# Weights made on VectorE in a fixed plan, with raw words two pieces ahead, in a fused attention and Fourier mixing kernel

## The chip, the cores and the metric

The kernel runs on one core of one Trainium2 chip. The metric is the time of one execution in device microseconds; lower is better. Before the change the median of three runs is 930.02 us (928.06 to 930.32).

## The reference

```python
def _attn_ref(q, k, v):                     # (4, 8, 768, 64) each
    block, window = (32, 16)
    scale = 1.0 / np.sqrt(D)
    k_sum = k.reshape(B, H, nb, block, D).max(axis=3)
    v_sum = v.reshape(B, H, nb, block, D).mean(axis=3)
    scores_l = scale * np.matmul(q, k.transpose(0, 1, 3, 2))
    mask_l = np.abs(pos[:, None] - pos[None, :]) < window
    scores_s = scale * np.einsum('bhsd,bhnd->bhsn', q, k_sum) + np.log(block)
    ...
    return np.matmul(softmax, np.concatenate([v, v_sum], axis=2))

def _moe_ref(x, w_ch1, w_ch2):              # x (4, 768, 512)
    mixed = np.real(np.fft.fft(np.fft.fft(x, axis=1), axis=2))
    u = x + mixed
    un = (u - mean(u)) / np.sqrt(var(u) + 1e-06)
    ch = np.maximum(un @ w_ch1, 0.0) @ w_ch2
    return u + ch                           # w_ch1 (512, 2048), w_ch2 (2048, 512)
```

The output of the attention, with the heads side by side, is the x of the mixing. The two weight matrices are stored as 64-bit floats; q, k and v are fp32.

## The kernel before, in words

There are four batches. For each one the kernel runs an attention (generator `gen_attention`, four pairs of heads), a Fourier stage (`gen_fourier`) and a channel stage (`gen_channel`). The attention of the next batch runs beside the Fourier and channel stages of the present one: `drive` (L956) takes steps from several generators in turn and so sets the order in which instructions are recorded; a scheduler then sets the order on each engine. Engines work through their own order, and so does SP, whose queue issues nearly all transfers.

**Attention.** `load` (L534) brings q and k of a head pair, 128 tokens to a tile, token p of tile t on partition p, so each packet is 64 floats. `prepare` (L582) transposes them on PE (L590) and copies them out of PSUM on ACT (L591). `scores` and `values` do the windowed part; `load_values` (L559) brings the windows of v, and on every second pair starts `block_sums` (L543), which brings the blocks of v and adds them on POOL through `gtt` (L528, its instructions carry L529).

**Fourier stage.** Additions on DVE fold x into the tile `fold`; matmuls with cosine and sine tables give y (L786), copied out by ACT (L792) and DVE (L793); matmuls mx (L806, L808) finish the transform; DVE adds x and takes mean and variance; an integer guess and four Newton steps give the inverse root (L823); DVE makes un (L833); PE transposes it (L837) into u, copied by DVE and ACT in turn (L838).

**Channel stage.** Both matrix products use a seven-product scheme of the Strassen kind: each operand is cut into four blocks, and four sums of blocks are added to it, so that a weight slab has seven parts (`_left_sums` L456 and `_right_sums` L463 make the sums). There are eight left slabs (w1, from w_ch1) and eight right slabs (w2, from w_ch2). In two chunks of four, `gen_channel` (L844) first makes h for each slab j (matmuls hx, hy, hz on L863; copies on ACT L870, L876, L878; additions on DVE through `tt`, L525, whose instructions carry L526; relu on DVE L867 and ACT L888), then multiplies h and its sums s with four right slabs for three pairs of row tiles (ox, oy, oz on L906, additions to x on DVE).

**Weights.** Batch 0 makes the slabs; batches 1 to 3 fetch them. `convert` (L678) turns 64-bit words into fp32, a half slab (a piece) at a time: it brings the raw words (L683; the tag raw has two buffers), takes exponent and mantissa apart on DVE (L687, L688), scales both on ACT (L689, L690), joins sign and low word on DVE (L691, L693), and multiplies the two parts on POOL. `make_w1` and `make_w2` convert two pieces, make the four sums on POOL and store the slab in DRAM (L706, L717), from where `get_w1` and `get_w2` (L722, L727) fetch it in later batches. `gen_weights` (L730) goes through four left slabs, four right ones, the other four left and the other four right. Three slabs are recorded after the whole attention of batch 0, the other thirteen beside its Fourier and channel stages, one slab to every four steps of those.

## Time and profile before

| | |
|---|---|
| median of 3 runs | 930.02 us |
| the profiled execution's own time | 931.02 us |
| its span in the profile | 929.2 us |
| mean granted TensorE clock | 0.94 |
| busy: PE, DVE, ACT, POOL | 829.2, 530.3, 168.8, 147.4 us |
| moved by DMA | 122.76 MB in 127,917 packets |

Engines: PE is TensorE's matmul, PEld its weight load, DVE VectorE, ACT ScalarE, POOL GpSimd, SP the queue of transfers. A group's row gives line, engine, operation, output<-inputs by the program's names, partitions x elements, the count, then total busy us and mean ns, and after the next bar the idle time before them with what ended it. A row of waits gives total us, times, and the longest. A row of windows gives, for one stretch, each engine's busy us with its instructions, the granted clock, the DMA share and GB/s.

### The profile page before, as it was taken

How to read it: one execution, taken by the hardware profiler on the slowest of the kernel's cores; microseconds unless marked ns; L12 is line 12 of the kernel's file. 1: busy time of each engine (PE TensorE's matmuls, PEld its weight loads, DVE VectorE, ACT ScalarE, POOL GpSimd, SP SyncE). 2: the span in 40 equal slices, each digit the busy share in tenths (PEclk: the TensorE clock that was granted, in tenths of full speed). 3: DMA queues.
4: the chain of work that ended last, by engine and by line, in shares of the span. 5: the costliest groups of instructions: out<-in, count | busy, mean ns of one | idle time of the engine just before them, and what ended most of it. 6: DMA issues, size and time to landing. Idle time of an engine off the chain costs nothing.

```text
span 929.2 us, 15289 instructions
## 1 busy us (share of the span) xinstructions
PE 829.2 (89%) x6386; PEld 618.3 (67%) x6386; DVE 530.3 (57%) x1158; ACT 168.8 (18%) x349; POOL 147.4 (16%) x142
## 2 busy tenths in 40 slices
PE   4778748687886799999999999999999997999997
PEld 3656634466753588657875888668857875587586
DVE  1366986799368964935423937635327556352252
ACT  2222312432023102221112012220021011200200
POOL 2230625567056700020000000000000000000000
PEclk9777859989898999999999999999999998999999
DMA  9995791777926508826162147321051161213101
GB/s 187 178 189 164 236 178 62 219 228 218 163 76 244 199 35 287 151 97 147 35 206 78 57 150 232 86 80 41 27 197 60 46 261 54 105 41 153 45 24 48
DMA packets 127917, 122.76 MB, mean 132 GB/s; under 512 B 102912, under 2 KB 111328, under 8 KB 127840
## 3 DMA queue, kind: packets, MB, share of 16 engines
q1 hardware_dynamic: 127296, 121.14, 46.9%
q8 instruction: 52, 0.85, 0.4%
q10 hardware_dynamic: 544, 0.56, 0.2%
q14 instruction: 25, 0.20, 0.1%
HBM read 100.71 MB, written 20.97 MB: 131 GB/s over the span
## 4 chain that ended last, share of the span: by engine, by line
PE 68%; DVE 20%; DMA 4%; POOL 3%; issue 3%; SPq 2%; ACT 1%; DVEq 0%; ACTq 0%; POOLq 0%
PE ox L906 17%; PE hx L863 15%; PE oz L906 8%; PE hz L863 7%; PE oy L906 4%; PE hy L863 4%; PE y L786 3%; DMA raw<-in_moe_w_ch_dram 2%; DVE cvt L688 2%; POOL w L529 2%; DVE cvt L693 2%; PE sc L606 2%; DVE cvt L691 2%; DVE x L526 2%; DVE cvt L687 2%
## 5 line engine op out<-in xcount | busy, mean ns | idle before, releaser
L863 PE MATMUL hx<-u,w 128*128 128x384 f32 x512 | 189.2, 500 | 15.5 <-ACT h L876 6.0
L863 PEld LDWEIGHTS hx<-u,w 128*128 128x128 f32 x512 | 97.9, 195 | 85.8 <-ACT h L876 8.9
L906 PE MATMUL ox<-w,h 128*128 128x256 f32 x384 | 93.9, 393 | 8.4 <-DVE x L526 7.9
L863 PE MATMUL hz<-u,w 128*128 128x384 f32 x256 | 96.6, 498 | 4.7 <-ACT h L878 4.7
L906 PE MATMUL ox<-w,s 128*128 128x256 f32 x384 | 92.8, 384 | 4.0 <-DVE x L526 3.5
L906 PE MATMUL oz<-w,s 128*128 128x256 f32 x384 | 93.0, 384 | 2.6 <-DVE s L526 2.6
L906 PEld LDWEIGHTS ox<-w,h 128*128 128x128 f32 x384 | 75.4, 197 | 22.8 <-DVE x L526 9.1
L906 PEld LDWEIGHTS ox<-w,s 128*128 128x128 f32 x384 | 72.0, 191 | 16.3 <-DVE x L526 5.6
L526 DVE TENSOR_TENSOR x<-ox,x 128x256 f32<-128x256 f32 x96 | 40.4, 422 | 74.2 <-PE ox L906 74.2
L906 PEld LDWEIGHTS oz<-w,s 128*128 128x128 f32 x384 | 73.3, 192 | 13.1 <-DVE s L526 2.9
L863 PEld LDWEIGHTS hz<-u,w 128*128 128x128 f32 x256 | 49.8, 195 | 40.3 <-POOL vb L529 5.3
L529 POOL TENSOR_TENSOR w<-cvt 128x512 f32<-128x512 f32 x32 | 43.6, 1364 | 133.2 <-DVE cvt L693 72.5
L529 POOL TENSOR_TENSOR w<-w 128x256 f32<-128x256 f32 x64 | 56.2, 893 | 3.1
L526 DVE TENSOR_TENSOR h<-hy,h 128x384 f32<-128x384 f32 x32 | 17.8, 555 | 67.5 <-PE hy L863 67.5
L526 DVE TENSOR_TENSOR h<-hx,h 128x384 f32<-128x384 f32 x32 | 17.8, 555 | 56.1 <-PE hx L863 56.0
L863 PE MATMUL hy<-u,w 128*128 128x384 f32 x128 | 46.5, 486 | 0.0
L906 PE MATMUL oy<-w,h 128*128 128x256 f32 x192 | 46.0, 380 | 0.3 <-POOL w L529 0.3
L606 PEld LDWEIGHTS sc<-qt,kt 64*64 64x64 f32 x1536 | 33.7, 157 | 12.7 <-issue 8.6
L606 PE MATMUL sc<-qt,kt 64*64 64x32 f32 x1536 | 36.7, 239 | 6.0 <-issue 3.7
L906 PEld LDWEIGHTS oy<-w,h 128*128 128x128 f32 x192 | 36.5, 191 | 5.8 <-POOL w L529 0.7
L867 DVE TENSOR_SCALAR h<-h 128x384 f32<-128x384 f32 x96 | 38.7, 404 | 2.9
L526 DVE TENSOR_TENSOR s<-h 128x512 f32<-128x512 f32 x48 | 39.2, 816 | 0.2
(92 smaller groups left out, 1043.3 us busy)
## 6 DMA issues: line engine op xcount, KB each, us to landing
w<-dw SPq DMA_DIRECT2D x48, 896.0 KB, 5.6
raw<-in_moe_w_ch_dram SPq DMA_DIRECT2D x32, 512.0 KB, 5.1
dw<-w SPq DMA_DIRECT2D x16, 896.0 KB, 4.3
vw<-in_v_dram SPq DMA_DIRECT2D x62, 192.0 KB, 5.7
kn<-in_k_dram SPq DMA_DIRECT2D x32, 192.0 KB, 5.3
qn<-in_q_dram SPq DMA_DIRECT2D x32, 192.0 KB, 5.2
vb<-in_v_dram SPq DMA_DIRECT2D x16, 384.0 KB, 6.3
out_dram<-x SPq DMA_DIRECT2D x24, 256.0 KB, 2.0
```

The source lines that it names most:

```text
L526: nc.vector.tensor_tensor(out=out, in0=in0, in1=in1, op=op)
L529: nc.gpsimd.tensor_tensor(out=out, in0=in0, in1=in1, op=op)
L606: nc.tensor.matmul(ps[h][r:r + 64, i, :], kt[rows, o:o + 64], qt[rows, o:o + BLOCK], start=True, stop=True)
L687: nc.vector.tensor_scalar(out=ex, in0=high, scalar1=0x7FF00000, scalar2=None, op0=ALU.bitwise_and)
L688: nc.vector.tensor_scalar(out=man, in0=high, scalar1=0x000FFFFF, scalar2=None, op0=ALU.bitwise_and)
L691: nc.vector.scalar_tensor_tensor(out=ex, in0=high, scalar=-(1 << 31), in1=ex, op0=ALU.bitwise_and, op1=ALU.bitwise_or)
L693: nc.vector.scalar_tensor_tensor(out=tmp[:, 1, :], in0=low, scalar=2.0 ** -52, in1=tmp[:, 1, :], op0=ALU.mult, op1=ALU.add)
L786: nc.tensor.matmul(y, fgs[par][:, st, P * g:P * (g + 1)], fs[par][:, g % 2, st, :], start=(st == 0), stop=(st == HT - 1))
L863: nc.tensor.matmul(ps, w[:, a, kk, :], u[:, r, kk, :], start=start and kk == 0, stop=stop and kk == 1, skip_group_check=True)
L867: nc.vector.tensor_scalar(out=t, in0=t, scalar1=0.0, scalar2=None, op0=ALU.max)
L906: nc.tensor.matmul(ps, left[a][:, n, :], wt[2, b, j][:, r, :], start=start and n == 0, stop=stop and n == NC - 1, skip_group_check=True)
```

## The change

The multiplication that ends a conversion and the four sums of each slab go from POOL to DVE. The sixteen slabs follow a written plan; some entries wait for a named step of the channel stage to be recorded. Raw words go through four buffers, which v's blocks share, and are loaded up to two pieces ahead of the piece in work. Left slabs are made in place; right slabs 0 to 3 are made in four small buffers of the tag s, stored, and fetched again when the channel stage of batch 0 comes to them. Weight steps now run beside the attention of batch 0 as well.

Around it: q and k are loaded with six consecutive tokens on a partition, one transfer for both heads, three pairs ahead, with twice as many copies on ACT behind the transposes; v's blocks are loaded one pair earlier; the two divisions per half in `values` become one; the second copy of y goes to ACT; the inverse root takes three shorter Newton steps; every second un goes to ACT; the first three left slabs of a batch are fetched in the Fourier stage; in batch 0 the relus go to ACT.

```diff
     def load(b, g):
-        qn, kn = (apool.tile([P, NST, 2, D], FP, tag="nat", bufs=4, name=f"{n}n_{b}_{g}") for n in "qk")
+        qn, kn = (apool.tile([P, 2, NST * D], FP, tag="nat", bufs=4, name=f"{n}n_{b}_{g}") for n in "qk")
         for dst, src in ((kn, k), (qn, q)):
-            for e in range(2):
-                nc.sync.dma_start(out=dst[:, :, e, :], in_=src[b, 2 * g + e].rearrange("(t p) d -> p t d", p=P))
+            nc.sync.dma_start(out=dst, in_=src[b, 2 * g:2 * g + 2].rearrange("e (p t) d -> p e (t d)", p=P))
...
-        raw = [bpool.tile([4 * nb, hf, D], FP, tag="vb", bufs=2, name=f"vb_{b}_{gg}_{i}") for i in range(2)]
+        raw = [bpool.tile([4 * nb, hf, D], FP, tag="raw", bufs=4, name=f"vb_{b}_{gg}_{i}") for i in range(2)]
...
-            for h in range(2):
-                ps = abank([P, HT, P], f"qk_{b}_{g}_{h}")
+            for e in range(2):
+                ps = abank([P, S2], f"qk_{b}_{g}_{e}")
                 for i in range(HT):
-                    nc.tensor.transpose(ps[:, i, :], src[:, HT * h + i].rearrange("p e d -> p (e d)"), ident)
-                nc.scalar.copy(out=dst[:, S2 * h:S2 * (h + 1)], in_=ps.rearrange("p i c -> p (i c)"))
+                    nc.tensor.transpose(ps[:, i::HT], src[:, e, P * i:P * (i + 1)], ident)
+                for par in range(2):
+                    nc.scalar.copy(out=dst[D * e:D * (e + 1), par:S:2], in_=ps[D * par:D * (par + 1)])
...
+    plan = [(1, 0, False, None), (1, 1, False, None), (2, 0, True, None), (1, 2, False, None), (2, 1, True, None),
...
+    def load_raw(upto):
+        for f, j, hh in pieces[len(raws):upto]:
+            raw = bpool.tile([P, 2 * HD, 2], I32, tag="raw", bufs=4, name=f"raw_{f}_{j}_{hh}")
...
+    def convert(piece, dst):
+        i = pieces.index(piece)
+        load_raw(i + 3)
+        raw = raws[i]
...
-        gtt(dst, vb, va, ALU.mult)
+        tt(dst, tmp[:, 1, :], tmp[:, 0, :], ALU.mult)
+        yield
...
+    def make(f, j, staged):
+        if staged:
+            t = [bpool.tile([P, n, HD], FP, tag="s", bufs=5, name=f"m{f}_{j}_{i}") for i, n in enumerate((2, 2, 2, 1))]
...
-        _left_sums(gtt, lambda i: w[:, i])
-        nc.sync.dma_start(out=dw1[j], in_=w)
+            yield from convert((f, j, hh), pair(hh).rearrange("p a n -> p (a n)"))
+        (_left_sums if f == 1 else _right_sums)(tt, part)
+        yield
...
-                nc.vector.tensor_copy(out=tr[:, g, par:S2:2], in_=ps[:, F2:0:-1])
+                nc.scalar.copy(out=tr[:, g, par:S2:2], in_=ps[:, F2:0:-1])
...
-            for _ in range(4):
-                tt(z, y, y, ALU.mult)
+            for _ in range(3):
+                nc.vector.scalar_tensor_tensor(out=z, in0=y, scalar=-0.5, in1=y, op0=ALU.mult, op1=ALU.mult)
                 tt(z, z, var, ALU.mult)
...
+            if t % 2:
+                nc.scalar.activation(out=un[:, t, :], in_=x[:, t, :], func=AF.Identity, bias=shift[:, i:i + 1],
+                                     scale=y[:, i:i + 1])
...
                 def relu(t):
-                    nc.vector.tensor_scalar(out=t, in0=t, scalar1=0.0, scalar2=None, op0=ALU.max)
+                    if b:
+                        nc.vector.tensor_scalar(out=t, in0=t, scalar1=0.0, scalar2=None, op0=ALU.max)
+                    else:
+                        nc.scalar.activation(out=t, in_=t, func=AF.Relu)
...
-    drive((gen_attention(0), 1))
+    attn, weights = gen_attention(0), gen_weights()
+    drive((first(attn, 5), 1), (first(weights, 15), 3))
     get_tables(0)
-    drive((gen_weights(0, 3), 1))
+    drive((attn, 1), (first(weights, 21), 3))
     for b in range(B):
-        gens = [(gen_post(b), 4)]
+        attn = gen_attention(b + 1) if b + 1 < B else iter(())
         if b == 0:
-            gens.append((gen_weights(3, None), 1))
-        if b + 1 < B:
-            gens.append((gen_attention(b + 1), 1))
-        drive(*gens)
+            drive((gen_fourier(0), 4), (first(weights, 20), 4), (first(attn, 5), 1))
+            drive((gen_channel(0), 4), (weights, 12), (attn, 1))
+        else:
+            drive((gen_post(b), 4), (attn, 1))
```

In the changed kernel the DVE lines of a conversion are L714, L715, L719 and L721, the ACT lines L716 and L717; transfers are L701 (raw), L749 and L752 (stores of staged and in-place slabs), L766 and L773 (fetches). `drive` now spreads the steps of its generators evenly over a round.

More of the change, by code (lines that the diff above doesn't have):

```diff
@@ L720, in get_w1, with gen_weights @@
+    def gen_weights():
+        for f, j, staged, stage in plan:
+            while stage and stage not in issued:
+                yield
+            yield from make(f, j, staged)
     def get_w1(b, j):
         w = bpool.tile([P, 7, 2, P], FP, tag="w1", bufs=3, name=f"w1_{b}_{j}")
+        if b == 0 and (1, j) not in made:
+            return
         nc.sync.dma_start(out=w, in_=dw1[j])
@@ L726, in get_w2 @@
         w = bpool.tile([P, 7, HD], FP, tag="w2", bufs=NC, name=f"w2_{b}_{j}")
+        if b == 0 and (2, j) not in made:
+            return
         nc.sync.dma_start(out=w, in_=dw2[j])
         wt[2, b, j] = w
-    def gen_weights(first, last):
-        steps = [(f, j) for c in range(0, NJ, NC) for f in (make_w1, make_w2) for j in range(c, c + NC)]
-        for f, j in steps[first:last]:
-            f(j)
-            yield
     tables = {}
```

129 lines of the change are left out of this document (81 added, 48 removed).

## The prediction

> **What bounds the kernel now.** I read the page's engine totals and its forty slices first, then the windows by stage, then who waits for whom inside the slowest stage.
>
> ```profile
> span 929.2 us, 15289 instructions
> PE 829.2 (89%) x6386; PEld 618.3 (67%) x6386; DVE 530.3 (57%) x1158; ACT 168.8 (18%) x349; POOL 147.4 (16%) x142
> ...
> PE   4778748687886799999999999999999997999997
> ...
> PEclk9777859989898999999999999999999998999999
> ```
>
> PE is the bound over the span, but not evenly: from slice 15 on it is full, and before that it is neither full nor at full clock. The windows are cut at the end of the first batch's attention (60), at the first channel matmul (137), at the first Fourier matmul of batches 1 to 3 (351, 550, 745) and at the end.
>
> ```profile
> core 0: us, PE busy (x) PEld busy (x) DVE busy (x) ACT busy (x) POOL busy (x), PEclk, DMA share, GB/s
> 0.00:60.00 60.00, 39.74 (x975) 32.45 (x976) 16.77 (x57) 15.39 (x33) 13.48 (x18) 0.86 1.04 184
> 60.00:137.00 77.00, 53.08 (x629) 43.12 (x629) 63.79 (x148) 21.50 (x43) 28.06 (x27) 0.67 0.81 196
> 137.00:351.00 214.00, 176.53 (x939) 123.52 (x939) 164.02 (x255) 50.54 (x92) 100.02 (x92) 0.92 0.55 158
> 351.00:550.00 199.00, 195.27 (x1575) 146.42 (x1574) 104.97 (x254) 31.55 (x71) 5.86 (x6) 1.00 0.46 127
> 550.00:745.00 195.00, 193.14 (x1584) 144.33 (x1583) 102.04 (x256) 29.98 (x67) 0.00 (x0) 1.00 0.33 106
> 745.00:929.00 184.00, 171.43 (x692) 128.47 (x690) 78.72 (x193) 19.81 (x43) 0.00 (x0) 0.97 0.24 92
> ```
>
> Batches 1 to 3 hold 3.7 + 1.9 + 12.6 us in which PE is idle; little can be won there. The first 351 us are the stage that can move. Its channel mixing is measured against that of batch 1, by the first channel matmul (hx) and the first Fourier matmul of the next batch (y):
>
> ```profile
> 137.21 1.67 PE L863 MATMUL hx<-u,w 128*128 128x384 f32 x4
> 350.62 1.48 PE L786 MATMUL y<-fs,fold 128*128 128x193 f32 x8
> 389.29 1.46 PE L863 MATMUL hx<-u,w 128*128 128x384 f32 x4
> 549.03 1.48 PE L786 MATMUL y<-fs,fold 128*128 128x193 f32 x8
> ```
>
> That is 213.4 us in batch 0 against 159.7 us in batch 1 for the same matmuls and the same share of the next batch's attention. So 53.7 us of batch 0's channel stage are the price of making the weights beside it. Who is waited for there, PE first, then the DMA queue, then DVE:
>
> ```profile
> PE ox L906 <- DVE x L526: 11.3, 4, 3.8
> PE hx L863 <- ACT h L876: 6.0, 2, 4.0
> ```
> ```profile
> SPq L717 <- POOL w L529: 48.2, 8, 10.7
> SPq L706 <- POOL w L529: 47.5, 5, 17.9
> ```
> ```profile
> DVE cvt L687 <- DMA raw<-in_moe_w_ch_dram: 9.1, 3, 4.4
> DVE cvt L687 <- POOL w L529: 3.4, 2, 1.7
> ```
>
> PE waits for additions and copies on DVE and ACT, which stand in line behind conversions. The DMA queue spends 95.7 us of the 214 waiting for POOL's sums before a store, with the next raw words behind it. POOL also slows DVE itself. Of the four conversion operations on DVE the trace gives minimum, median and maximum:
>
> ```profile
> L687 DVE TENSOR_SCALAR cvt<-raw x32: 412/587/1485, 85.8 to 311.8; 128x512 int32<-128x512 int32 x32
> L688 DVE TENSOR_SCALAR cvt<-raw x32: 413/946/1502, 86.2 to 312.2; 128x512 int32<-128x512 int32 x32
> L691 DVE SCALAR_TENSOR_TENSOR cvt<-raw,cvt x32: 669/680/2835, 87.2 to 313.1; 128x512 int32<-128x512 int32 x32
> L693 DVE SCALAR_TENSOR_TENSOR cvt<-raw,cvt x32: 677/679/2836, 87.8 to 313.7; 128x512 f32<-128x512 uint32 x32
> ```
>
> The fast ones stand where POOL is idle, the slow ones where it computes. The same operation of 0.41 us takes up to 1.5.
>
> **The change part by part.** First the work that goes from POOL to DVE.
>
> ```profile
> L529 POOL TENSOR_TENSOR w<-w 128x256 f32<-128x256 f32 x64 | 56.2, 893 | 3.1
> L529 POOL TENSOR_TENSOR w<-cvt 128x512 f32<-128x512 f32 x32 | 43.6, 1364 | 133.2 <-DVE cvt L693 72.5
> L689 ACT ACTIVATE cvt<-cvt,rebias 128x512 int32<-128x512 int32 x32 | 23.1, 722 | 82.7 <-DVE cvt L687 82.6
> L690 ACT ACTIVATE cvt<-cvt 128x512 f32<-128x512 int32 x32 | 20.0, 626 | 7.3 <-DVE cvt L688 5.0
> L526 DVE TENSOR_TENSOR x<-ox,x 128x256 f32<-128x256 f32 x96 | 40.4, 422 | 74.2 <-PE ox L906 74.2
> ```
> The next two views are groups by form on DVE, in batch 1 (POOL nearly idle) and in 137 to 351:
> ```profile
> L526 DVE TENSOR_TENSOR s<-h 128x512 f32<-128x512 f32 x12 | 8.2, 684 | 0.1
> ```
> ```profile
> L691 DVE SCALAR_TENSOR_TENSOR cvt<-raw,cvt 128x512 int32<-128x512 int32 x24 | 23.0, 959 | 0.4 <-ACT cvt L689 0.4
> L688 DVE TENSOR_SCALAR cvt<-raw 128x512 int32<-128x512 int32 x24 | 22.8, 951 | 0.0
> L693 DVE SCALAR_TENSOR_TENSOR cvt<-raw,cvt 128x512 f32<-128x512 uint32 x24 | 20.9, 869 | 0.0
> L687 DVE TENSOR_SCALAR cvt<-raw 128x512 int32<-128x512 int32 x24 | 17.9, 744 | 12.4 <-DMA raw<-in_moe_w_ch_dram 9.1 <-POOL w L529 3.4
> L526 DVE TENSOR_TENSOR s<-h 128x512 f32<-128x512 f32 x12 | 14.6, 1214 | 0.0
> L867 DVE TENSOR_SCALAR h<-h 128x384 f32<-128x384 f32 x24 | 12.8, 539 | 0.5
> ```
>
> A piece costs DVE (23.0+22.8+20.9+17.9)/24 = 3.52 us now. With POOL quiet it is 0.41+0.41+0.67+0.68 = 2.17, plus the multiplication that comes over, for which the nearest row is 0.684 (same width): 2.85 us. A slab (two pieces, four sums of 128x256; nearest row 0.422, from PSUM) is 5.7 + 1.7 = 7.4 us. Sixteen slabs are 118 us, against 32 x 3.52 = 113 now: DVE takes over 99.8 us of POOL's work at about no cost of its own, if the quiet prices hold. They hold as far as POOL is quiet: only the block sums of v stay there.
>
> The Trainium skill, Perfetto Trace Analysis, section Optimizing Scalar/DVE Operations, speaks both ways: work of a saturated DVE may be moved to ScalarE or even GPSIMD, which is the reverse of this change, but those two share a port and the move might not help. SBUF — State Buffer, section SBUF: two separate sides, makes that port an exclusive lock held for a whole instruction; the 0.41 to 1.50 us of one operation agree with the lock. By the first half alone the change would only add load, the slower rival below.
>
> DVE in batch 0's channel stage. The first rows are from before, a right slab between additions (in raw_2_1_1331 the slab, its piece, a buffer's number):
>
> ```order
> L687 TENSOR_SCALAR cvt_2_0_1323<-raw_2_0_1321 128x512
> L688 TENSOR_SCALAR cvt_2_0_1323<-raw_2_0_1321 128x512
> L867 TENSOR_SCALAR h_0_1521<-h_0_1521 128x384 x2
> L691 SCALAR_TENSOR_TENSOR cvt_2_0_1323<-raw_2_0_1321,cvt_2_0_1323 128x512
> L693 SCALAR_TENSOR_TENSOR cvt_2_0_1323<-raw_2_0_1321,cvt_2_0_1323 128x512
> L687 TENSOR_SCALAR cvt_2_1_1333<-raw_2_1_1331 128x512
> L688 TENSOR_SCALAR cvt_2_1_1333<-raw_2_1_1331 128x512
> L526 TENSOR_TENSOR h_0_1521<-hy_3_1841,h_0_1521 128x384
> ```
> The same engine and stage of the changed kernel, left slab 3 between the additions of step 1:
> ```order
> L526 TENSOR_TENSOR w_0_3_1556<-cvt_1559 128x512
> L721 SCALAR_TENSOR_TENSOR cvt_1658<-raw_3_1_1354,cvt_1658 128x512
> L526 TENSOR_TENSOR h_0_1526<-hy_1_1648,h_0_1526 128x384
> L526 TENSOR_TENSOR w_0_3_1556<-cvt_1658 128x512
> L526 TENSOR_TENSOR w_0_3_1556<-w_0_3_1556 128x256 x4
> L714 TENSOR_SCALAR cvt_1692<-raw_4_0_1557 128x512
> L715 TENSOR_SCALAR cvt_1692<-raw_4_0_1557 128x512
> L526 TENSOR_TENSOR h_0_1526<-hx_1_1647,h_0_1526 128x384
> ```
> The relus have gone to ACT, the multiplications and sums have come in, and an addition that PE waits for can stand behind a whole run of sums (four, 1.7 us).
>
> The DMA queue on SP in the same stage, before (raw words of slabs 5 and 6, stores dw):
> ```order
> L683 DMA raw_5_0_1667<-in_moe_w_ch_dram 128x4x256
> L683 DMA raw_5_1_1677<-in_moe_w_ch_dram 128x4x256
> L538 DMA qn_0_1947<-in_q_dram 128x6x64
> L706 DMA dw_4_90<-w_0_4_1538 128x1792
> L683 DMA raw_6_0_1775<-in_moe_w_ch_dram 128x4x256
> ```
> The changed kernel's queue, same slabs; w<-dw fetches a staged right slab:
> ```order
> L701 DMA raw_5_0_1690<-in_moe_w_ch_dram 128x4x256
> L773 DMA w_0_2_1756<-dw_2_96 128x1792
> L701 DMA raw_5_1_1767<-in_moe_w_ch_dram 128x4x256
> L752 DMA dw_4_90<-w_0_4_1689 128x1792
> L701 DMA raw_6_0_1801<-in_moe_w_ch_dram 128x4x256
> L538 DMA kn_1_1842<-in_k_dram 128x2x384
> ```
> A store still has raw words behind it, but it now waits for DVE, which needs those words only after more of its own work, with four raw buffers instead of two. The 95.7 us of waiting for POOL lose their cause; what is late next is a raw piece behind v's block sums, which share the four buffers. The q and k lines change from pieces of 64 to pieces of 384 floats (256 B to 1,536 B).
>
> Channel stage of batch 0. By the order, nine slabs are left for it (before: twelve): 9 x 7.4 = 66.6 us. DVE's other work is 164.0 - 84.6 - 12.8 (relus) - 6.4 (s at its quiet price) = 60.2 us. Together 127 us beside 159.7 us of PE: DVE no longer sets the pace on average. A piece also waits for ACT in its middle (0.72 + 0.63 us), mostly under other DVE work. PE idles now 214 - 176.5 = 37.5 us there; bounds for what is left are 0 and 37.5. I take 13, about a third, since DVE is 80% loaded in a fixed order. So 160 + 13 = 173 us against 213.4.
>
> Up to the first hx. DVE: other work 80.6 - 8 x 3.52 = 52 us, less some 5 for copies and norms that went to ACT or shrank; seven slabs instead of four: 52 us. With the first 9 us, in which nothing has landed, DVE could be there at 108. DMA: counted by the shapes in the new order, 33 MB stand ahead (q and k 7.1, v windows 5.5, v blocks 3.1, raw 8.4, stores 6.4, tables and constants 2.5) where 26 MB (60 x 184 + 77 x 196) ran before. The rates lie between the small pieces (184 GB/s at a share of 1.04 in 0:60) and the large ones:
>
> ```profile
> 280.00:300.00 20.00, 11.64 (x31) 6.46 (x30) 17.89 (x22) 7.56 (x14) 12.85 (x12) 0.87 0.76 272
> ```
> 272/0.76 = 358 GB/s. v's windows stay small, 31 us; the other 27.5 MB need 77 to 149 us, nearer the first since no piece among them is below 1 KB. That is 108 to 180 us. With both engines near 110 and a chain of Fourier steps behind the attention, I take 128 against 137.2.
>
> The Trainium skill, DMA: Bandwidth & Descriptors, section Specifications, puts the least size for full rate at 512 B; by it the low end, 108 us, would stand. No row here shows a size between 256 B and 1 KB apart.
>
> Batches 1 to 3. Half of the un steps and one copy per y go to ACT, three Newton steps replace four, fetches of w stand earlier, and eight ACT copies replace four per head pair (0.5 us each, hidden under PE). In batch 3, with no attention as cover:
> ```profile
> PE unt L837 <- DVE norm L526: 4.0, 1, 4.0
> ```
> Of 12.6 us idle I take 4 off (bounds 9 off, 3 added).
>
> The sum: 350.6 becomes 128 + 173 = 301, so -49.6, and -4: 53.6 off the profiled execution's 931.0 us (span 929.2) is 877.4. That run lies 1.0 above the median of 930.0, so 876 us.
>
> **The rivals.**
> Faster, 851 us: DVE and DMA both near their floors, first hx at 114 and a channel stage of 162, so 276 instead of 301. For it: the loads worked out above, 108 and 127 us. Against it: fixed in-order queues on three engines that wait for each other.
> Transfers hold the start, 914 us: if 33 MB run at the mean of the first 137 us (26.1 MB/137 = 191 GB/s), the first hx is at 173, 45 later than taken, less 7 as more slabs can then be ready. For it: share 1.04 now. Against: larger pieces.
> Slower, 941 us: DVE becomes the bound because its operations keep their crowded prices. Channel stage: 9 x (7.04 + 1.37 + 1.7) = 91, other work 66.6, waits for ACT 18 x 1.35 = 24, waits for PE as now (214 - 164.0, less the 12.5 for raw words and POOL) 37.5: 219. Start: 7 x 10.1 + 47 + 9 + 14 x 1.35 = 146. That is 365 instead of 350.6, with 4 off as above. It decides once DVE's work and waits pass 350 us, that is, if L715 again averages 0.95 us. Against it: POOL has almost nothing left to collide with.
>
> **How the numbers follow.** A measurement of this kernel tells 0.3% (2.8 us) from no change. Forecast 876 (862 to 898): 0.66. Faster rival: 0.17. Transfers: 0.11. Slower rival: 0.04; gains and losses that cancel: 0.02. The range 848 to 900 holds the forecast's bounds and most of the faster rival; beyond it lie the transfer rival and the slower one. Faster 0.94, same 0.02, slower 0.04.
>
> **What would show it.** Right: L714 and L715 near 0.42 us, POOL busy below 50 us, first hx of batch 0 near 128, y of batch 1 near 301, PE idle in between near 13 us, no SP waits for POOL's weight sums. Wrong: a first hx later than 145, a channel stage above 190 us, DVE waits for raw words of more than 10 us, or batches 1 and 2 longer than 199 and 195.

## The result, and the profile after

The changed kernel takes 900.8 us (median of four, 897.8 to 904.3) beside 929.0 us for the kernel before: a ratio of 0.970, 95% interval 0.965 to 0.974. Measured once more in a later group (e2_control below) it was 896.3 us, 0.9645 (0.9608 to 0.9681). Two measurements of one kernel thus lie 0.5% apart, and no smaller difference is read below. The forecast was 876 us, so somewhat more than half of the 54 us forecast came (28 us between these medians, 32 between the profiled executions). The profiled execution took 898.64 us with a span of 896.8.

The engine totals and the forty slices, on the page after:

```profile
span 896.8 us, 15260 instructions
PE 829.4 (92%) x6386; PEld 615.5 (69%) x6386; DVE 500.8 (56%) x1106; ACT 231.1 (26%) x481; POOL 49.4 (6%) x46
...
PE   4785889899997998999999998999999988999997
...
PEclk9755787999999999999999999999999999999999
```

PE is at 7 tenths or more from slice 5 on and nearly full from slice 7, where it was full from slice 15 before. POOL fell from 147.4 to 49.4 us, ACT rose from 168.8 to 231.1. The granted clock is low in slices 2 to 7, and nowhere later. The windows, cut at the end of batch 0's attention, at the first hx, and at the first y of batches 1 to 3:

```profile
core 0: us, PE busy (x) PEld busy (x) DVE busy (x) ACT busy (x) POOL busy (x), PEclk, DMA share, GB/s
0.00:82.80 82.80, 55.02 (x1016) 42.24 (x1020) 47.57 (x101) 36.66 (x70) 17.83 (x21) 0.73 1.01 249
82.80:146.90 64.10, 51.81 (x590) 40.03 (x583) 53.85 (x131) 26.67 (x59) 6.83 (x5) 0.74 0.76 194
146.90:316.40 169.50, 159.84 (x913) 114.31 (x912) 132.29 (x260) 57.85 (x112) 24.15 (x18) 0.99 0.61 182
316.40:516.20 199.80, 196.54 (x1597) 146.46 (x1596) 96.69 (x222) 44.98 (x98) 0.63 (x2) 1.00 0.41 124
516.20:715.00 198.80, 195.55 (x1588) 145.10 (x1587) 96.65 (x225) 40.98 (x90) 0.00 (x0) 1.00 0.32 105
715.00:896.80 181.80, 170.67 (x694) 127.32 (x692) 73.75 (x170) 23.92 (x54) 0.00 (x0) 0.98 0.25 93
```

And the rows that set the cuts, as in the prediction:

```profile
146.94 1.46 PE L905 MATMUL hx<-u,w 128*128 128x384 f32 x4
...
316.37 1.48 PE L825 MATMUL y<-fs,fold 128*128 128x193 f32 x8
```

| | before | forecast | after |
|---|---|---|---|
| first hx of batch 0 | 137.2 | 128 | 146.9 |
| channel stage of batch 0 (hx to y of batch 1) | 213.4 | 173 | 169.4 |
| first y of batch 1 | 350.6 | 301 | 316.4 |
| y of batch 1 to the end | 578.6 | 574.6 | 580.4 |

The channel stage gave 44 us, more than forecast. The start took 9.7 us where 9 were to be gained, and batches 1 to 3 took 1.8 where 4 were to be gained: -44.0 + 9.7 + 1.8 = -32.5, which is the 32.4 us between the two profiled executions. Of the 21 us that are missing from the forecast's 53.6, 19 lie ahead of the first hx, 6 behind y of batch 1, and 4 came back in between.

The four conversion operations on DVE, with minimum, median and maximum, and what SP's queue waited for up to the first hx:

```profile
L714 DVE TENSOR_SCALAR cvt<-raw x32: 385/419/432, 24.9 to 266.3; 128x512 int32<-128x512 int32 x32
L715 DVE TENSOR_SCALAR cvt<-raw x32: 411/421/2581, 25.3 to 266.6; 128x512 int32<-128x512 int32 x32
L719 DVE SCALAR_TENSOR_TENSOR cvt<-raw,cvt x32: 670/692/1732, 28.0 to 271.5; 128x512 int32<-128x512 int32 x32
L721 DVE SCALAR_TENSOR_TENSOR cvt<-raw,cvt x32: 679/684/1754, 29.4 to 272.7; 128x512 f32<-128x512 uint32 x32
```
```profile
SPq L749 <- DVE m L526: 17.5, 2, 13.7
SPq L752 <- DVE cvt L714: 10.7, 1, 10.7
SPq L701 <- DVE cvt L721: 10.5, 4, 5.2
SPq L749 <- DVE norm L526: 6.1, 1, 6.1
SPq L548 <- DVE cvt L714: 5.0, 1, 5.0
```

The medians are the quiet prices that the forecast used. SP no longer waits for POOL's sums, but it stands before stores (L749, L752) and raw buffers (L701, L548) until DVE has got to them, with v's windows and q and k behind. PE's waits up to the first y of batch 0 begin with these:

```profile
PE av L640 <- DMA vw<-in_v_dram: 7.9, 2, 6.2
PE y L825 <- DVE fold L810: 6.4, 1, 6.4
PE ss L622 <- DVE km L594: 5.2, 1, 5.2
PE qk L591 <- DMA kn<-in_k_dram: 5.0, 1, 5.0
```

The fold that follows the first attention thus begins at 82.8 us, where it began at 59.7 before the change.

### The profile page after: what moved, and what is told of

Same layout as the page of the kernel before. It is cut to its first block, busy times and chain, and to the rows that moved or that the text cites. A ratio compares the mean times of both kernels' runs of the same rounds, so it can differ in the third digit from the quotient of the medians.

```text
span 896.8 us, 15260 instructions
## 1 busy us (share of the span) xinstructions
PE 829.4 (92%) x6386; PEld 615.5 (69%) x6386; DVE 500.8 (56%) x1106; ACT 231.1 (26%) x481; POOL 49.4 (6%) x46
## 5 line engine op out<-in xcount | busy, mean ns | idle before, releaser
L905 PE MATMUL hx<-u,w 128*128 128x384 f32 x512 | 187.3, 496 | 7.0 <-DVE h L526 4.2
L905 PE MATMUL hz<-u,w 128*128 128x384 f32 x256 | 93.9, 486 | 0.0
L952 PE MATMUL ox<-w,h 128*128 128x256 f32 x384 | 89.6, 380 | 0.6 <-DMA w<-dw 0.6
L952 PEld LDWEIGHTS ox<-w,h 128*128 128x128 f32 x384 | 72.7, 190 | 12.1 <-DMA w<-dw 0.8
L831 ACT COPY big<-y 128x192 f32<-128x192 f32 x32 | 10.7, 334 | 140.1 <-PE y L825 140.0
L825 PE MATMUL y<-fs,fold 128*128 128x193 f32 x192 | 37.7, 346 | 6.9 <-DVE fold L810 6.4
L915 ACT COPY h<-hx 128x384 f32<-128x384 f32 x32 | 15.3, 478 | 100.7 <-PE hx L905 96.4
L825 PEld LDWEIGHTS y<-fs,fold 128*128 128x128 f32 x192 | 32.8, 198 | 10.6 <-DVE fold L810 6.6
```

The lines of the kernel that those rows point to most:

```text
L825: nc.tensor.matmul(y, fgs[par][:, st, P * g:P * (g + 1)], fs[par][:, g % 2, st, :], start=(st == 0), stop=(st == HT - 1))
L831: nc.scalar.copy(out=ty[:, g, par:S2:2], in_=y[:, 0:F2])
L905: nc.tensor.matmul(ps, w[:, a, kk, :], u[:, r, kk, :], start=start and kk == 0, stop=stop and kk == 1, skip_group_check=True)
L915: nc.scalar.copy(out=c11, in_=X)
L952: nc.tensor.matmul(ps, left[a][:, n, :], wt[2, b, j][:, r, :], start=start and n == 0, stop=stop and n == NC - 1, skip_group_check=True)
```

## The experiments

Three theories for the late start. Theory 1: the DMA engines carry too many bytes ahead of the first hx. Theory 2: SP's queue stands on stores and raw buffers, and the attention's loads stand behind. Theory 3: conversions on DVE, their steps on ACT and the doubled q and k copies stand between the attention's own steps on these engines. All kernels are edits of the changed kernel, and each ratio is to the kernel before on the same chip.

A scheduler sets the final order on every engine, and each edit moves some of it. The mark "first hx" suffers from that: where PE reaches hx early, the order has often pushed one or two head pairs of the next attention behind it. So the first y of batch 1, which needs all of that attention, is the better mark. The score matmuls (sc) inside batch 0's channel stage, of the changed kernel and of e1_one_op, show such a push, 96 against 288 of the 384. The end of the first attention is read by one mark too, the start of the fold on DVE that follows it: 82.8 us in the changed kernel, 79.0 in the control below.

```profile
L608 PE MATMUL sc<-qt,kt 64*64 64x32 f32 x96 | 1.6, 220 | 0.0
```
```profile
L608 PE MATMUL sc<-qt,kt 64*64 64x32 f32 x288 | 6.1, 238 | 3.4 <-issue 3.4
```

**First group: which of the three.** Stores from another queue (e1_stores_pool):

```
-                nc.sync.dma_start(out=to[:, 2 * i:2 * i + n], in_=t[i])
+                nc.gpsimd.dma_start(out=to[:, 2 * i:2 * i + n], in_=t[i])
...
-            nc.sync.dma_start(out=to, in_=wv)
+            nc.gpsimd.dma_start(out=to, in_=wv)
```

> The changed kernel, with the stores of finished slabs issued from POOL's queue in place of SP's, so that q, k and v loads no longer stand behind a store that waits for DVE. Measured by the first channel matmul of batch 0 (hx, 146.9 us in the changed kernel) and by the end of the first attention (82.1). Queue order (theory 2: SP stood 10.7 us in front of one store ahead of the fold, 17.5 + 6.1 us behind it): hx at 130 to 138, time about 888. Transfers (theory 1: the bytes are the same): hx within 3 us of 147, time 898. Engines (theory 3: conversions and copies beside the attention lengthen it): within 3 us of 147.

Measured: 890.0 us, 0.9556 (0.9529 to 0.9582), first hx at 137.5, y of batch 1 at 307.9. PE's wait for v's windows ahead of the first y fell from 7.9 to 1.8 us, but the fold began at 79.4, no earlier than in the control: what was gained lies behind it. By y of batch 1 theory 2 holds for some 8 us.

More bytes (e1_more_bytes), in the function that loads the raw words:

```
+            if len(raws) < 14:
+                dup = dpool.tile([64, 4 * HD], I32, name=f"dup_{len(raws)}")
+                nc.sync.dma_start(out=dup, in_=moe_w_ch2.bitcast(I32)[64 * len(raws):64 * (len(raws) + 1), :])
```

> The changed kernel with 14 more copies of 256 KB each, from the weights' rows to a scratch in DRAM that nothing reads, one behind each of the first 14 loads of raw words (3.67 MB). Transfers (theory 1): at the 236 to 274 GB/s of the first 93 us this is 13 to 16 us more, hx at 160, time about 912. Queue order (theory 2) and engines (theory 3): nothing waits for these copies, hx at 147 to 150.

Measured: 895.3 us, 0.963 (0.9599 to 0.966), first hx at 133.2, y of batch 1 at 314.5. The window of its first attention:

```profile
0.00:82.00 82.00, 50.99 (x1012) 39.47 (x1012) 42.41 (x101) 36.34 (x69) 16.98 (x21) 0.74 1.05 277
```

The copies were carried beside the rest, at 277 GB/s where the changed kernel moved 249, and the fold began at 82.0. The 13 to 16 us of theory 1 did not come. PE's wait for v's windows did grow, from 7.9 to 10.8 us: a single load can be late although the bytes are not the limit.

q and k as before the change (e1_old_qk): the load, transposes and copies of the diff taken back.

> The changed kernel with loads of q and k and their transposes and copies as before (256-B pieces, four ACT copies per head pair in place of eight). Transfers (theory 1): 7.1 MB at 184 in place of about 255 GB/s, 11 us more, hx at 155 to 160. Queue order (theory 2): four DMAs in place of two per pair in the same order, hx within 3 us of 147. Engines (theory 3): ACT's copies were 2.1 us in a chain at each pair and are halved, hx 3 to 8 us earlier. Batches 1 to 3 (580.4 us in the changed kernel, 578.6 before): if the copies took the 4 us that were forecast to be gained, 575 to 577; if not, 580.

Measured: 887.8 us, 0.9546 (0.9502 to 0.9589); first hx at 131.8, y of batch 1 at 317.0, from there to the end 568.0. The pieces of 256 B do cost something in the first attention: PE waits 15.3 us there for k and 13.4 for v's windows, in place of 5.0 and 7.9, and the fold begins at 86.6. By y of batch 1 that is made up, and behind it the old form is shorter, so the new loads and copies of q and k are a loss of about 1% of their own.

One operation in place of a conversion (e1_one_op):

```
         low, high = raw.bitcast(U32)[:, :, 0], raw[:, :, 1]
+        if i < 14:
+            yield
+            yield
+            nc.vector.tensor_scalar(out=dst, in0=low, scalar1=2.0 ** -52, scalar2=None, op0=ALU.mult)
+            yield
+            return
```

> The changed kernel with the first 14 pieces (7 slabs) not converted: one multiplication on DVE writes the words scaled, so the weights are not the reference's. Same loads, sums and stores; DVE has 14 x 2.2 = 31 us less before hx, ACT 14 x 1.35 = 19 us less. Transfers (theory 1): hx within 4 us of 147. Queue order (theory 2): the stores wait shorter, hx at 135 to 140. Engines (theory 3): attention ends at 62 to 68 in place of 82, hx at 120 to 128.

Measured: 887.0 us, 0.9527 (0.9508 to 0.9547); first hx at 121.5, y of batch 1 at 308.6. The fold began at 77.8, near the control's 79.0, and the attention did not end at the 62 to 68 of theory 3: without the conversions it is hardly shorter. PE waits 8.7 us for k and 9.0 for v's windows in it, DVE 10.8 us for raw words. Behind the fold DVE's share does show:

```profile
77.80:121.50 43.70, 39.44 (x474) 32.22 (x471) 34.41 (x95) 18.25 (x42) 5.11 (x5) 0.89 0.82 214
```

The early hx came in part from the push shown above; y of batch 1 came 8 us early.

**Second group: the control, both gains, and the two large parts taken back.** e2_control is the changed kernel unedited.

> The changed kernel once more, unedited, on the chip and beside the runs of this group: 898 to 904 us, first hx near 147, y of batch 1 near 316. All theories expect this; a value below 893 would mean that the gains of the first group are a difference of chips.

Measured: 896.3 us, 0.9645 (0.9608 to 0.9681), hx at 146.2, y at 316.4.

e2_stores_oldqk joins the edits of e1_stores_pool and e1_old_qk.

> The changed kernel with both edits of the first group that gained: stores of slabs from POOL's queue (889.98) and q and k as before the change (887.77). If the two causes are separate places (SP's queue before y of batch 1, ACT's copies in the later Fourier stages), the gains add: 11 + 13 off 901, 877. If both only free SP's queue or only shift the order, they overlap: 886 to 890.

Measured: 882.5 us, 0.9519 (0.9469 to 0.9569), y of batch 1 at 308.0, from there 572.0. It is 14 us under its control and the fastest version here that makes the reference's weights. The gains add in part: the 8 us ahead of y are the stores', 7 of the others stayed.

The weights taken out from beside the attention (e2_attn_first):

```
-    drive((first(attn, 5), 1), (first(weights, 15), 3))
+    drive((attn, 1))
     get_tables(0)
-    drive((attn, 1), (first(weights, 21), 3))
+    drive((first(weights, 36), 3))
```

> The changed kernel with the steps of the weights taken out from beside the first attention: 36 steps (six slabs) after it, in place of 15 and 21 in it. Queue order and engines (theories 2 and 3, in both the weights lengthen the attention): last x row of the attention at 56 to 62 in place of 80; the six slabs then take 6 x 7.4 = 44 us of DVE beside the Fourier steps, hx at 130 to 147, time 885 to 902. Transfers (theory 1): the bytes only move behind, the attention ends no earlier than 72, hx at 147 or later. Beside that: if PE's granted clock follows its own idle time, 0 to 60 is again near 0.86, where it was 0.78.

Measured: 909.6 us, 0.977 (0.9733 to 0.9807). The windows up to its fold, and from there to its first hx:

```profile
0.00:64.90 64.90, 45.16 (x976) 34.64 (x976) 20.83 (x53) 27.92 (x55) 16.69 (x21) 0.84 1.02 207
64.90:162.50 97.60, 61.50 (x787) 49.07 (x788) 78.00 (x185) 41.41 (x84) 6.67 (x5) 0.72 0.72 214
```

The fold behind the attention alone begins at 64.9 us, 14 to 18 before that of the changed kernel (79.0 in the control, 82.8 in the first run), so this is what the weights beside it cost. Made afterwards they cost more: the stretch from the fold to hx is 34 us longer (97.6 against 64.1, with all of the next attention's scores in it), and y of batch 1 comes at 330.2, 14 us later. To make them beside the attention is right, and is not free. First hx (162.5) and time lie beyond the 130 to 147 and 885 to 902 us of theories 2 and 3, whose end of the attention came near; the clock of the first window, 0.84, is near the 0.86 that was expected.

The sums back on POOL (e2_sums_pool): `tt` becomes `gtt` for the last multiplication and for the four sums of a slab.

> The changed kernel with multiplications and sums of the weights on POOL again, all else as changed. If the move to DVE is what made the channel stage of batch 0 shorter (213 to 169 us): L714 and L715 back to 0.75 to 0.95 us, that stage at 195 to 215 us, time 925 to 945. If the new order, four raw buffers and staging did it: stage 165 to 180, time 895 to 910.

Measured: 911.0 us, 0.9797 (0.9767 to 0.9828), channel stage 194.9 us (135.0 to 329.9, with 288 of the score matmuls in it). Both lie between the two forecasts. There, by form, and then two of the rows in the changed kernel's stage:

```profile
L719 DVE SCALAR_TENSOR_TENSOR cvt<-raw,cvt 128x512 int32<-128x512 int32 x19 | 19.8, 1043 | 3.0 <-ACT cvt L716 3.0
L721 DVE SCALAR_TENSOR_TENSOR cvt<-raw,cvt 128x512 f32<-128x512 uint32 x19 | 13.7, 723 | 0.0
L714 DVE TENSOR_SCALAR cvt<-raw 128x512 int32<-128x512 int32 x18 | 13.4, 743 | 3.0 <-POOL w L529 3.0
L715 DVE TENSOR_SCALAR cvt<-raw 128x512 int32<-128x512 int32 x18 | 12.3, 686 | 0.0
```
```profile
L715 DVE TENSOR_SCALAR cvt<-raw 128x512 int32<-128x512 int32 x18 | 7.6, 421 | 0.0
L714 DVE TENSOR_SCALAR cvt<-raw 128x512 int32<-128x512 int32 x18 | 7.6, 421 | 0.0
```

The crowded prices are back as soon as POOL works beside DVE (743 and 686 ns against 421). The move from POOL to DVE is worth 15 us of the time (911.0 against 896.3). By y of batch 1 it is 13.5 of the 34 us that the change gained up to there (350.6, 329.9, 316.4); the other 21 belong to the rest of the change, the new order, the staging and the buffers among it, whose parts were not taken back one by one. The 25 us between the two channel stages (194.9 and 169.5) hold the push as well.

**Third group: how far each goes, and the clock.** The raw words too from POOL's queue (e3_weights_pool):

> The changed kernel with the loads of raw words too on POOL's queue, beside the stores of slabs: SP keeps q, k, v, tables and fetches alone. Queue order (theory 2): with POOL's queue for the stores alone y of batch 1 came at 308 in place of 316; now SP waits neither for raw buffers nor for stores, attention ends at 65 to 72, y of batch 1 at 295 to 303, time 875 to 885, if POOL's block sums of v, which stand in the same queue now, are not late. If what is left of the start is engines and clock (theory 3): y at 305 to 310, time 886 to 892.

Measured: 892.2 us, 0.9576 (0.9553 to 0.9598), fold at 88.2, y of batch 1 at 310.7. The attention ended later, and not 65 to 72. The last matmuls of its values began at 78.0, but their divisions stood on DVE behind conversions that had themselves waited for raw words:

```profile
82.72 0.43 DVE L714 TENSOR_SCALAR cvt<-raw 128x512 int32<-128x512 int32 x1 [3.00 <-DMA raw<-in_moe_w_ch_dram]
...
86.74 0.26 DVE L649 RECIPROCAL rec<-av 128x6 f32<-128x6 f32 x2
86.97 1.02 DVE L526 TENSOR_TENSOR x<-av,rec 128x384 f32<-128x384 f32 x2
```

SP still waited for raw buffers before v's blocks (4.5 us). So this kernel moves the wait from SP's queue to DVE's, and does not tell what a free SP queue alone is worth.

e3_one_op_stores joins e1_one_op and e1_stores_pool.

> The changed kernel with both: the first 14 pieces made by one operation each (the weights are not the reference's) and the stores on POOL's queue. Alone they gave y of batch 1 at 308.6 and 307.9. If SP's queue waits because DVE is late with slabs (one cause), the gains overlap: 304 to 308, time 882 to 887. If the conversions hold the start by themselves (theory 3) beside the queue, they add: 298 to 302, time 872 to 879.

Measured: 874.2 us, 0.9379 (0.9355 to 0.9402).

```profile
296.18 0.98 PE L831 MATMUL y<-fs,fold 128*128 128x193 f32 x5
```

The two causes add, to 20 us: y of batch 1 at 296, below the 301 that was forecast for the kernel with all its conversions. The fold still began at 78.1, with PE's waits of 8.7 us for k and 6.6 for v's windows ahead of it. The gain lies behind the fold:

```profile
78.10:125.10 47.00, 39.84 (x525) 32.66 (x522) 36.92 (x104) 18.42 (x42) 11.87 (x17) 0.94 1.08 296
```

DVE has 36.9 us of work between fold and hx, where the changed kernel has 53.9, and PE's clock is 0.94 in place of 0.74.

Eight copies from the old layout (e3_oldqk_8copies): the q and k of e1_old_qk, with each copy cut in two.

```
-                nc.scalar.copy(out=dst[:, S2 * h:S2 * (h + 1)], in_=ps.rearrange("p i c -> p (i c)"))
+                for e in range(2):
+                    nc.scalar.copy(out=dst[D * e:D * (e + 1), S2 * h:S2 * (h + 1)],
+                                   in_=ps[D * e:D * (e + 1)].rearrange("p i c -> p (i c)"))
```

> The changed kernel with loads and transposes of q and k as before the change, but each of the four ACT copies per head pair cut in two by partitions: eight copies of 64x384 as in the changed kernel, from the old layout. If the number of copies on ACT is what batches 1 to 3 pay for the q and k part (580 us, 568 with the old loads and four copies): 577 to 581, time 895 to 901. If the layout (strided writes and reads, the load's order) is the cause: 567 to 573, time 886 to 890.

Measured: 891.5 us, 0.9579 (0.9553 to 0.9606), between the two; behind y of batch 1 571.6 us, as the layout theory had it. PE's idle time in that stretch is the finer measure: 17.6 us in the changed kernel and in its control, 15.2 here, 11.0 with the old loads and four copies. So the number of copies is worth some 4 us of it and the layout some 2. The rest of the 12 us is work of PE done ahead of the stretch: these two kernels have 672 score matmuls left in it, where the changed kernel has 768. With 768 and four copies (e2_stores_oldqk) PE idles for 12.2 us.

More work for PE (e3_keep_clock), called behind the scores, behind the sum scores and ahead of the values of each head pair:

```
+    def fill(b, g, i, qt):
+        for n in range(3 if b == 0 else 0):
+            nc.tensor.matmul(bank([P, S2], f"fill_{g}_{i}_{n}"), ident, qt[:, 0:S2], start=True, stop=True)
```

> The changed kernel with 36 matmuls more (128x384, 0.486 us each at full clock, 17.5 us in all), nine beside each head pair of the first attention, on operands that are there already; nobody reads them. DVE, ACT and SP keep their order. If the low granted clock of the first 80 us (0.78, then 0.60) comes of PE's idle time: clock 0:80 at 0.85 to 0.95, the attention ends within 4 us of 80 in spite of the added work, time 893 to 904. If the clock is low for another reason: PE's added work takes 17.5/0.7 = 25 us, of which the 28 idle us take some half, attention at 90 to 95, time 908 to 915.

Measured: 908.8 us, 0.9766 (0.9745 to 0.9786), fold at 90.9. The first 80 us, of the changed kernel and of this one:

```profile
0.00:80.00 80.00, 52.22 (x928) 39.71 (x932) 44.77 (x95) 36.36 (x69) 17.83 (x21) 0.73 1.00 249
```
```profile
0.00:80.00 80.00, 63.45 (x880) 42.83 (x880) 35.66 (x87) 34.28 (x65) 10.58 (x16) 0.91 0.88 217
```

The clock went from 0.73 to 0.91 with nothing but matmuls added to the program, inside the range that was given if it follows PE's own idle time. The time and the end of the attention came as the other theory had them: the fold began 8 to 12 us later, with 17.5 us more work. So the clock follows PE's idle time, and filling the gaps did not pay.

**Fourth group: which engine, and the copies.** ACT's two steps left out of the first 14 pieces (e4_no_act); every second q and k copy on DVE (e4_split_copies); that with the stores on POOL's queue (e4_stores_split). In the expectations of this group and the next, "the kernel before" is the one named just ahead:

```
+        if i >= 14:
+            nc.scalar.activation(out=ex, in_=ex, func=AF.Relu, bias=rebias, scale=8.0)
+            nc.scalar.activation(out=tmp[:, 1, :], in_=man, func=AF.Copy, bias=1.0, scale=2.0 ** -20)
```
```
-                    nc.scalar.copy(out=dst[D * e:D * (e + 1), par:S:2], in_=ps[D * par:D * (par + 1)])
+                    (nc.vector.tensor_copy if par else nc.scalar.copy)(
+                        out=dst[D * e:D * (e + 1), par:S:2], in_=ps[D * par:D * (par + 1)])
```

> The changed kernel, in whose first 14 pieces ACT's two steps are left out (19 us of ACT, and DVE's wait for them, 8.9 us before hx; the weights are not the reference's); DVE's five operations stay. If ACT's turn in the middle of a piece holds the start: y of batch 1 at 305 to 310, time 885 to 890, as with one operation for all. If DVE's 31 us of work hold it: y at 313 to 317, time 894 to 901.

> The changed kernel with every second of the eight q and k copies per head pair on DVE. If the queue on ACT is what the q and k part costs: PE's wait for ACT in the un steps of batches 1 to 3 falls from 5.0 to about 2 us, batches 1 to 3 take 572 to 576, time 888 to 895. If the layout is: 578 to 581, and DVE's 13 us more beside the weights can make batch 0 later, time 896 to 905.

> As the kernel before, and the stores of slabs from POOL's queue. Queue on ACT: both gains, 878 to 884. Layout: no better than the stores alone, 888 to 893.

Measured: e4_no_act 896.6 us, 0.9621 (0.9586 to 0.9656), y of batch 1 at 314.6: ACT's turn held nothing that shows, and of what e1_one_op left out DVE's part remains. e4_split_copies 898.4 us, 0.964 (0.9603 to 0.9676): PE's wait for ACT in the un steps fell from 5.0 to 2.2 us and PE's idle time behind y of batch 1 from 17.6 to 13.9; that stretch took 577.9, but y of batch 1 went to 318.8. e4_stores_split 898.5 us, 0.9653 (0.9625 to 0.9681), y at 318.4: the stores' gain is gone. Its start:

```profile
0.00:83.70 83.70, 55.70 (x1016) 43.92 (x1020) 54.52 (x121) 27.09 (x50) 20.16 (x27) 0.73 1.06 258
83.70:146.70 63.00, 44.95 (x498) 36.16 (x491) 58.16 (x140) 23.06 (x50) 12.59 (x18) 0.77 0.81 221
```

DVE is busy for 58 of the 63 us behind the fold. Where it is loaded by 11 us more up to the first hx (112.7 against 101.4 us), a freer SP queue brought nothing.

**Fifth group: DVE relieved in the start alone.** The last multiplication and the sums of the first 14 pieces on POOL, the others on DVE (e5_pool_start); that with the old q and k (e5_pool_start_oldqk); that with the stores on POOL's queue as well (e5_pool_start_stores_oldqk):

```
-        tt(dst, tmp[:, 1, :], tmp[:, 0, :], ALU.mult)
+        (gtt if i < 14 else tt)(dst, tmp[:, 1, :], tmp[:, 0, :], ALU.mult)
...
-        (_left_sums if f == 1 else _right_sums)(tt, part)
+        (_left_sums if f == 1 else _right_sums)(gtt if pieces.index((f, j, 0)) < 14 else tt, part)
```

> The changed kernel with multiplications and sums of the first seven slabs only on POOL (14 x 0.68 + 28 x 0.42 = 21 us less on DVE before hx), the later nine on DVE as changed. If DVE's work holds the start: y of batch 1 at 304 to 311, time 884 to 892, the channel stage of batch 0 still 167 to 172. If POOL's collisions cost DVE as much as it is relieved of (L714, L715 of the start at 0.7 in place of 0.42 us): y at 314 to 320, time 896 to 903.

> As the kernel before, with q and k loaded and prepared as before the change. If the causes are separate: 8 to 13 us less than the kernel before, 872 to 882. If not: 884 to 890.

> As the kernel before, and the stores of slabs on POOL's queue, where those of the first seven slabs stand behind POOL's own sums and wait for nothing else. If SP's waits for stores still count: 866 to 876, the fastest of all. If they counted only because DVE was late with slabs: within 4 us of the kernel before.

Measured: 903.5 us, 0.9695 (0.9664 to 0.9725), with y of batch 1 at 325.4; 894.7 us, 0.961 (0.9594 to 0.9626); 892.2 us, 0.9595 (0.9574 to 0.9617). All three miss the times of their first theories. The old q and k take 8.8 us off beside POOL's work too, so that cause is separate, and the stores on POOL's queue take no more off that can be told (2.5 us). Up to the first hx of e5_pool_start, DVE's costliest groups:

```profile
L526 DVE TENSOR_TENSOR p<-p,near 128x384 f32<-128x384 f32 x12 | 10.8, 923 | 5.6 <-ACT p L612 5.6
L719 DVE SCALAR_TENSOR_TENSOR cvt<-raw,cvt 128x512 int32<-128x512 int32 x13 | 10.5, 810 | 4.2 <-ACT cvt L716 4.2
...
L715 DVE TENSOR_SCALAR cvt<-raw 128x512 int32<-128x512 int32 x14 | 7.5, 534 | 0.0
...
L714 DVE TENSOR_SCALAR cvt<-raw 128x512 int32<-128x512 int32 x14 | 6.4, 457 | 12.3 <-DMA raw<-in_moe_w_ch_dram 12.3
```

The attention's own multiplication by the mask (p) takes 923 ns beside a busy POOL, where it took 552 in the changed kernel, and DVE waits 12.3 us for raw words. POOL is no relief for DVE here, in the start as little as in the channel stage.

## Why the prediction was right and wrong, step by step

**The channel stage was right.** The quiet prices came (0.42 and 0.42 us in the median; the multiplications took 0.69 us apart from a few of up to 2.9, beside v's block sums on POOL), SP stopped waiting for POOL's sums, and DVE took 132.3 us there against a sum of 127, beside 159.8 us of PE. PE idles 9.7 us; 13 was forecast. The reason given, POOL's collisions, is shown by e2_sums_pool, but as one part of the gain: with POOL back at work y of batch 1 comes at 329.9, and not at 350.6.

**The step that failed** is the one that set the first hx: "With both engines near 110 and a chain of Fourier steps behind the attention, I take 128". It came at 146.9, and of the signs of being wrong that the prediction named, a first hx later than 145 and batches 1 and 2 longer than 199 and 195 (199.8 and 198.8) came. DVE's sum itself was good: 52 - 5 + 52 = 99 us were worked out, and 47.6 + 53.9 = 101.4 were measured. But a floor of an engine's total says when it could be done, and not when its work can be placed, and the forecast put at nothing what the weights do to the attention beside them. The fold began at 82.8 in place of 59.7, 23.1 us later; from the fold to hx it took 64.1 us in place of 77.5, 13.4 less. With the old start of the fold, the same 64.1 us would have ended at 124, ahead of the 128; but the two hang together, since a slab that is not made beside the attention has to be made behind it.

These are the marks, in us:

| | last av of the attention begins | fold begins | first y of batch 0 | y of batch 1 |
|---|---|---|---|---|
| before | 58.0 | 59.7 | 80.4 | 350.6 |
| changed | 79.3 | 82.8 | 92.8 | 316.4 |
| e2_control | 75.6 | 79.0 | 89.2 | 316.4 |
| e2_attn_first | 63.3 | 64.9 | 95.1 | 330.2 |
| e1_stores_pool | 72.6 | 79.4 | 89.5 | 307.9 |
| e1_one_op | 73.7 | 77.8 | 83.3 | 308.6 |
| e3_one_op_stores | 73.8 | 78.1 | 83.1 | 296.2 |
| e3_weights_pool | 78.0 | 88.2 | 93.2 | 310.7 |

*The attention.* Of the 23 us, 14 to 18 are the price of the weights beside it (e2_attn_first); the other 5 came with the rest of the change. The price has two parts. PE is idle for 27.8 us ahead of the fold (25.0 in the control) where it is for 19.7 without the weights; 7.9 (6.2) of that are waits for v's windows, which e2_attn_first does not have. And PE is busy for 55.0 us (54.0) where it was for 45.2, at a clock of 0.73 (0.72) where it was 0.84: by an estimate, busy time times clock, some 8 of these 9 to 10 us are the clock. Which queue makes PE wait is not settled: with one operation per piece, with the stores gone from SP, and with both, the fold still began at 78 to 79 us.

*Behind the fold.* DVE was busy 57% of the time ahead of it, where it waits for PE and ACT and they for it, and then 84%. At first it is more:

```profile
82.80:121.00 38.20, 31.30 (x314) 24.58 (x306) 35.02 (x75) 13.03 (x33) 6.83 (x5) 0.84 0.84 214
```

That is 35 of 38 us. So DVE had no slack where the Fourier steps wait for it, and idled where it had slack to lose. The first y waits for the fold's additions: it began 10.0 us behind the fold, and PE waited 6.4 us; with one operation per piece it was 5.5 us, and with the stores moved as well 5.0. PE's waits for them:

```profile
PE y L831 <- DVE fold L816: 2.6, 1, 2.6
```
```profile
PE y L831 <- DVE fold L816: 1.0, 1, 1.0
```

From the fold to y of batch 1 the changed kernel takes 234 us (237 in the control), e1_one_op 231, e1_stores_pool 229 and e3_one_op_stores 218. DVE's work alone is thus worth 3 to 7 us behind the fold, although e1_one_op has 19 us less of it there; only with the stores off SP's queue as well, and 17 us less for DVE, is it 16 to 19.

A second omission belongs to the same step. The forecast had no term for the clock, though the rows it quoted had 0.86 and 0.67 in them. PE's busy time by the granted clock, from the windows, is an estimate of its work at full clock: before 39.74 x 0.86 + 53.08 x 0.67 + 176.53 x 0.92 = 232 us of 351, after 55.02 x 0.73 + 51.81 x 0.74 + 159.84 x 0.99 = 237 of 316. The work is the same to 5 us. What the change saved is idle time (82 to 50 us), while the loss by the clock, 37 and 30 us, hardly moved: ahead of the first hx it even grew, from 23 us (92.8 busy, 69.7 of it at full clock) to 28 (106.8, 78.5). PE that idled in a stage paid a second time in the clock, which e3_keep_clock shows in reverse.

**Bytes do not hold the start.** The forecast's DMA ends (108 and 180 us) and the rival of 914 us rested on bytes over a rate. e1_more_bytes carried 3.67 MB more in the same time, so a share of 1.01 was no sign of a limit. When a single load lands is another matter: PE waited 12.9 us for k and for v's windows in the first attention of the changed kernel, and 28.7 with the old loads.

**Batches 1 to 3: -4 was forecast, +1.8 came** (+0.2 in the control, so nothing was gained). PE's idle time behind y of batch 1 fell from 18.4 to 17.6 us only. The un steps that went to ACT were to shorten PE's wait. PE's transposes in these batches, before, after, and with the old q and k (e1_old_qk):

```profile
L837 PE MATMUL unt<-ident,big 128*128 128x128 f32 x72 | 11.6, 318 | 9.3 <-DVE big L833 5.3 <-DVE norm L526 4.0
```
```profile
L882 PE MATMUL unt<-ident,big 128*128 128x128 f32 x72 | 9.6, 278 | 9.1 <-ACT big L875 5.0 <-DVE norm L860 3.9
```
```profile
L881 PE MATMUL unt<-ident,big 128*128 128x128 f32 x72 | 11.3, 304 | 5.7 <-DVE norm L859 3.9 <-ACT big L874 1.8
```

The wait only changed its name: 5.3 us for DVE became 5.0 for ACT, which has the doubled q and k copies in its queue, and a Newton step less took 0.1 us off the other. With four copies the wait is 1.8 us, with eight from the old layout 4.6, and with half of the new copies on DVE 2.2. The step "eight ACT copies replace four per head pair (0.5 us each, hidden under PE)" failed here: PE hides them, but the next step on ACT stands behind them, and PE waits for that.

**What stays open.** Which queue lengthens the attention; and whether the stores' 8 us are SP's waiting or the order that the scheduler made with them: e1_stores_pool gained them, e3_weights_pool kept five or six, e4_stores_split lost them.

## What to carry to other kernels

An engine's total work gives a floor for a stage, not its time: before such a floor is used, look in which windows the engine is idle, and whether the moved work can stand there without standing in front of a step that another engine waits for. Work placed "beside" a chain of dependent steps on the same in-order queues can lengthen the chain, here from 65 to 79 or 83 us, by the estimate above about half of it through the lower clock that PE was granted. A step moved to a less loaded engine moves its wait with it, if that engine's queue is given other work in the same change.

## What the runs showed of the hardware

The granted clock follows PE's own gaps: 36 matmuls whose results nobody reads raised it from 0.73 to 0.91 over 80 us. The Trainium skill, TensorE: Matmul & The Clock Gate, Part 1: The HAM clock gate, says that the default state is throttled and activity releases it; the row of e3_keep_clock beside that of the changed kernel agrees.

A mean busy share of the DMA engines of 1.01 left room: at 1.05 they moved 277 GB/s where 249 had been moved, with 3.67 MB more in copies of 256 KB.

POOL's work slowed DVE operations that have no data in common with it: the mask's multiplication p (128x384) took 552 ns in the mean in the changed kernel and 923 ns in e5_pool_start, where POOL has multiplications and sums of the weights beside it. In the changed kernel one multiplication of a conversion began at 160.23 us, beside a sum of v's blocks on POOL (160.19, 2.34 us), and took 2.86 us in place of 0.69.
